# First GLU layer as 26 products of 4x4 by 4x2 blocks, with weight sums made during the first chunk and streamed from DRAM

## The chip, the core and the metric

The kernel runs on one core of a Trainium2 chip. The core has five engines that run side by side: TensorE (PE in the profile), VectorE (DVE), ScalarE (ACT), GpSimd (POOL) and SyncE (SP), which here only issues DMAs. Each engine works through its own queue strictly in order. The metric is the time of one execution on the device in microseconds, the median of several runs.

## The reference, cut to what matters

A linear attention block feeds a gated feed-forward layer, all in fp32 (the weights arrive as float64 and are converted on the chip).

```python
kv = np.einsum('bhsd,bhse->bhde', k, v)          # batch 8, heads 8, seq 576, head_dim 64
out = np.einsum('bhsd,bhde->bhse', q, kv)
out = out / sqrt(mean(out * out, -1) + 1e-6) * g_norm
x = out.transpose(0, 2, 1, 3).reshape(4608, 512)
gate = 1.0 / (1.0 + np.exp(-(x @ w_gate)))       # w_gate, w_val: 512 x 1536
val = x @ w_val
result = gate * val @ w_out                      # w_out: 1536 x 512
```

## The kernel before, in words

The 4608 tokens go through in nine chunks of 512 (G, NG). For each chunk c a first layer makes `h = sigmoid(gate) * val` and a second layer multiplies h with w_out. Everything lies in the transposed form that TensorE wants: xT holds 512 model dimensions as four tiles of 128 partitions, h holds 1536 hidden dimensions as twelve tiles.

**Chunk 0** (from the string `order` at L602 to L1096) starts the pipeline: eight pairs of heads of attention, the conversion of the weights (18 units, L156 to L211, five VectorE and two ACT instructions each: twelve "gv" units with a gate and a value tile, six "wo" units), and plain matmuls (`plain`, L583, and `second`, L669). In `plain` the conversion steps of the next unit are recorded between the matmuls of this one, so that TensorE waits for a unit only if VectorE is late.

**First layer of chunks 1 to 8** (`first_layer_fast`, L761). For each f of six, a gate and a value column tile and their partners f + 6 are treated as a 2x2 block product in Strassen-Winograd form: six products of two tiles and 256 tokens each on both partners, and the seventh again as a smaller such scheme of seven matmuls of 128x128. The sums of weights (tws, txs) are made on GpSimd in chunks 0 and 1 (`w_sum` L751, `w_sums2` L742), kept in DRAM and loaded again for each later chunk (`load_sums` L737). The sums of x (`x_sums` L702, `x_sums2` L712) are eight VectorE instructions a chunk.

**Second layer.** In chunk 1 it is plain (`second_layer_plain` L993), while VectorE makes 18 sums of w_out (`w_forms` L968). From chunk 2 on (`second_layer_fast` L1009) it is a scheme of 26 products (`PRODUCTS` L908), each a sum over three blocks j. Its left factors are 28 sums of h tiles per block (`H_SUMS` L899, `h_sums` L943, all on GpSimd), its right factors sums of w_out, streamed through a ring (`load_w` L964). The results are combined on VectorE and ACT as each product is done: `finish` (L1037) reads a small text such as `o5=o5-C`, in which capital letters are PSUM regions.

**PSUM banks.** Five banks circulate in a queue `free` (L540, `take` and `give`): a product that opens a region takes the oldest free bank, a region's last reader gives it back.

**The order around the change.** `fill` is a queue of single steps; `slot()` (L339) runs the next one. It is called at fixed places between products, seven times per f in the first layer and once per product in the second. In it lies the feed of attention for a later batch (`feed(b)`, L345, run during chunk b - 1): `kv_mm` (k and v products on TensorE, 40 of them), `kv_copies` on ACT, `turn` (VectorE transposes of q), and twice `two_pairs`: `u_mm` (TensorE), `u_square` (ACT), two `u_sum` (VectorE), `u_root` (ACT), two `u_norm` (VectorE, the first with a reciprocal that reads the root), two `x_turn` (VectorE transposes, each followed by DMAs on SP that place x in xT). `idle` steps and `spread` (L464) set the distances. After the feed come the x sums of the next chunk (`sums_of`, L1075). `load_late(b)` (L108) loads k and v of a batch into h_more, on SP, at the end of a second layer; in the kernel before, that of batch 2 is in the middle of chunk 0.

GpSimd's own queue holds the h sums, one addition per f, and the DMA issues of the weight sums and of the ring.

Of the kernel before, what the change touches and what calls it, by code (L numbers as in the profile page):

```python
# [10 lines left out]
FP32 = mybir.dt.float32  # L11
# [9 lines left out]
def kernel(  # L21
# [46 lines left out]
    NT = G // P  # L68

# [58 lines left out]
    units = [("gv", f) for f in range(NFT)] + [("wo", f) for f in range(0, NFT, 2)]  # L128
# [15 lines left out]

    def words(u):
        t = staged[u].rearrange("p i f -> p (i f)").bitcast(U32).rearrange("p (n two) -> p n two", two=2)
        return t[:, :, 0], t[:, :, 1]
# [8 lines left out]
    def convert(u):  # L156
# [4 lines left out]
        def s0():  # L161

            t = w1[:, f] if kind == "gv" else w2[:, f:f + 2, :]
            if kind == "gv":
                for i, name in enumerate(("wg", "wv")):
                    w[name, f] = t[:, i].rearrange("p (m f) -> p m f", m=NMT)
            else:
                for i in range(2):
                    w["wo", f + i] = t[:, i]
            d["m"] = m = t.rearrange("p i f -> p (i f)")  # L170
            vec.tensor_scalar(out=m.bitcast(U32), in0=words(u)[1], scalar1=0x000FFFFF, scalar2=None,
                              op0=ALU.bitwise_and)
# [5 lines left out]
        def s1():  # L178


            d["p"] = p = raw.tile([P, UW], U32, tag="cz", name="cz", bufs=2)
# [45 lines left out]
    w1 = const.tile([P, NFT, 2, DM], FP32, name="w1")  # L227
# [117 lines left out]
    def feed(b):  # L345

        early = b == 2
# [100 lines left out]
        if b > 2:  # L448
            steps += [(PE, idle)] * 6
        steps.append((PE, kv_mm))  # L450
        for i in range(2 * NC):
            for rs in ((0, 1), (2,)):
                steps.append((ACT, lambda i=i, rs=rs: kv_copies(i, rs)))

        u, *rest = two_pairs(n0)
        steps += turns_of(n0 + 1) + [u] + rest[:1] + [(PE, idle)] * (3 if b > 2 else 0) + turns_of(n0 + 2) + rest[1:]

        steps += [(PE, idle)] + turns_of(n0 + 3) + [(PE, idle)] * (2 if b > 2 else 0)
        return steps + two_pairs(n0 + 2) + [(PE, idle)] * 4
# [3 lines left out]

    def spread(steps, at):  # L464

        n = 0
        for engine, step in steps:
            while engine == DVE and n < 7 * NF2 and n % 7 not in at:
                fill.append(idle)
                n += 1  # L470
            fill.append(step)
            n += 1
# [6 lines left out]
    N3 = NF2 // 2  # L479
# [13 lines left out]

    def sg_tile():
        return sb.tile([P, G], FP32, tag="sg", name="sg", bufs=6)
# [87 lines left out]
    def plain(c, f, ps):  # L583

        blk = Plain(c, f, ps)
        for at in range(2 * NMT):
# [3 lines left out]
            convert_step(f + 1, at)  # L590
# [24 lines left out]
    for token in order.split():  # L615
# [3 lines left out]
        if name == "b":  # L619
            if f not in blks:  # L620
# [6 lines left out]
                blks[f] = Plain(0, f, ps)  # L627
# [9 lines left out]
        elif name == "M":  # L637
            nc.vector.tensor_tensor(out=gv_tile(0, f), in0=copies[f, 1], in1=copies[f, 0], op=ALU.mult)
# [11 lines left out]
        else:  # L650
            a[f][steps[name]]()
            if token == f"Q{NE - 1}":
# [3 lines left out]
                h_more = hp.tile([P, N3, 3 * NT, P], FP32, name="h_more")  # L656
    late.extend([blks[3].gate, blks[3].end])
    for f in range(4, NFT):
# [5 lines left out]
        if f == NFT - 2:  # L664
            load_late(2)
# [13 lines left out]
    raw_ctx.__exit__(None, None, None)  # L679

# [8 lines left out]
    NK = NMT // 2  # L689
    h1, h2 = slice(0, GH), slice(GH, G)  # L690
    tt = nc.vector.tensor_tensor
    sx, tw = {}, {}


    sx2, tw2 = {}, {}

    q1, q2 = slice(0, P), slice(P, GH)

    def quarters(c):
        return {(i, j): xT[c][:, NK * (j - 1):NK * j, GH * (i - 1):GH * i] for i in (1, 2) for j in (1, 2)}  # L700

    def x_sums(c):  # L702
        a = quarters(c)
        sx[c] = s = sums.tile([P, 3, NK, GH], FP32, tag="sx", name="sx", bufs=1)
        return [
            lambda: tt(out=s[:, 0], in0=a[2, 1], in1=a[2, 2], op=ALU.add),
            lambda: tt(out=s[:, 1], in0=s[:, 0], in1=a[1, 1], op=ALU.subtract),
            lambda: tt(out=a[2, 1], in0=a[1, 1], in1=a[2, 1], op=ALU.subtract),
            lambda: tt(out=s[:, 2], in0=a[1, 2], in1=s[:, 1], op=ALU.subtract),
        ] + x_sums2(c, a[1, 2])  # L710

    def x_sums2(c, a):  # L712
        sx2[c] = s = sums.tile([P, 3, P], FP32, tag="sx2", name="sx2", bufs=1)
        a11, a12, a21, a22 = a[:, 0, q1], a[:, 1, q1], a[:, 0, q2], a[:, 1, q2]
        return [
            lambda: tt(out=s[:, 0], in0=a21, in1=a22, op=ALU.add),
            lambda: tt(out=s[:, 1], in0=s[:, 0], in1=a11, op=ALU.subtract),
            lambda: tt(out=a21, in0=a11, in1=a21, op=ALU.subtract),
            lambda: tt(out=s[:, 2], in0=a12, in1=s[:, 1], op=ALU.subtract),
        ]  # L720

    def places(c, f):

        if c > 1 and f % 2 == 0:
            free_ = w1[:, :, 1, 0:NK * P]
            return free_[:, 0:8].rearrange("p (i e) n -> p i e n", e=2), free_[:, 8:10]
        return tws, txs

    def name_sums(c, f):
        t, x = places(c, f)  # L730
        for i in (1, 2, 3, 4):
            for e in range(2):
                tw[f + NF2 * e, i] = t[:, i - 1, e].rearrange("p (m c) -> p m c", m=NK)
            j, r = divmod(i - 1, 2)
# [403 lines left out]
```

## Time and profile before

| what | value |
|---|---|
| median of 3 runs | 1068.87 us (1067.32 to 1069.75) |
| the profiled execution | 1070.65 us, span 1068.8 us, granted TensorE clock 0.998 |
| VectorE, ACT, GpSimd busy | 600.7, 322.2, 504.3 us |
| chunk 0 | 0 to 160.2 us |
| chunk 1: first layer, plain second layer | 160.2 to 242.8, 242.8 to 284.0 us |
| chunks 2 to 6 | 284.0 to 851.0 us |
| chunks 7 and 8 (no feed in them) | 851.0 to 958.4, 958.4 to 1063.8 us |
| DMA | 184.5 MB, of it 119.6 MB on GpSimd's queue |

The page of the profile has one line of busy time per engine, then groups of instructions by source line, and the chain of work that ended last. The timeline lists start, duration, engine, source line, operation, tiles and count; a bracket at the end tells how long the engine stood idle before and what released it. Windows give busy time per engine in a stretch, in the order PE, PEld, DVE, ACT, POOL, then the granted clock and the DMA share. A matmul in fp32 appears as two records. Starts of TensorE records that follow each other without a gap show the rate; the duration of one record is longer, because they overlap.

### The profile page before, as it was taken

What the parts mean: (1) busy time and instruction counts of PE and PEld (TensorE: products, weight loads), DVE (VectorE), ACT (ScalarE), POOL (GpSimd) and SP (SyncE); (2) the same over time, 40 slices, a digit from 0 to 9 for tenths busy, and PEclk for the clock granted to TensorE, in tenths of its full rate; (3) what the DMA queues carried; (4) which work ended last, traced back from release to release, by engine and by line L of the source; (5) the groups of instructions that cost most, each with busy time, mean ns of one, the idle gap of its engine ahead of it and who ended that gap; (6) DMA issues with size and microseconds to landing.
All of it is one profiled execution on the core that took longest, in us unless ns stands there. A gap on an engine that the chain in (4) does not pass through costs nothing.

```text
span 1068.8 us, 19454 instructions
## 1 busy us (share of the span) xinstructions
PE 1052.3 (98%) x7334; PEld 858.2 (80%) x7334; DVE 600.7 (56%) x1340; ACT 322.2 (30%) x772; POOL 504.3 (47%) x972
## 2 busy tenths in 40 slices
PE   8999999999999999999999999999999999999998
PEld 7544448884688888888888788888888888888886
DVE  4887765566445555564557355555465555535542
ACT  4654324330142403331243224331334032202220
POOL 0000045782246842675166724682368427852762
PEclk9999999999999999999999999999999999999999
DMA  9944712346754686348733793358535833473214
GB/s 258 257 158 158 245 61 98 112 150 209 275 183 151 196 268 210 110 139 266 216 110 125 227 283 123 132 171 272 167 122 174 257 117 99 132 257 115 99 47 156
DMA packets 97533, 184.52 MB, mean 173 GB/s; under 512 B 29216, under 2 KB 68384, under 8 KB 94752
## 3 DMA queue, kind: packets, MB, share of 16 engines
q0 software_dynamic: 27168, 119.55, 33.6%
q1 hardware_dynamic: 70016, 63.66, 20.6%
q8 instruction: 58, 0.95, 0.4%
q14 instruction: 35, 0.29, 0.1%
q10 hardware_dynamic: 256, 0.07, 0.0%
HBM read 151.78 MB, written 24.38 MB: 165 GB/s over the span
## 4 chain that ended last, share of the span: by engine, by line
PE 87%; DMA 5%; POOL 4%; DVE 2%; issue 1%; ACT 0%; SPq 0%; POOLq 0%; DVEq 0%
PE mm L766 44%; PE mm L1034 15%; PE mm L571 7%; PE mm L770 7%; PE mm L999 4%; PE mm L670 4%; DMA xT<-xTs 3%; PE at L399 2%; PE at L358 1%; POOL tws L757 1%; POOL h_more L944 1%; DVE sg L1047 1%; PE at L571 1%; DMA w_ring<-kept 1%; PE two L295 1%
## 5 line engine op out<-in xcount | busy, mean ns | idle before, releaser
L766 PE MATMUL mm<-xT,w 128*128 128x256 f32 x720 | 177.5, 380 | 0.0
L766 PE MATMUL mm<-sx,w 128*128 128x256 f32 x720 | 177.1, 379 | 0.0
L766 PEld LDWEIGHTS mm<-xT,w 128*128 128x128 f32 x720 | 133.4, 190 | 17.7 <-issue 1.0
L766 PEld LDWEIGHTS mm<-sx,w 128*128 128x128 f32 x720 | 132.1, 190 | 15.2
L785 DVE TENSOR_TENSOR h<-mm,sg 128x256 f32<-128x256 f32 x96 | 40.8, 425 | 147.6 <-PE mm L766 147.6
L766 PE MATMUL mm<-sx,tws 128*128 128x256 f32 x432 | 111.1, 380 | 1.6 <-issue 1.6
L766 PE MATMUL mm<-xT,tws 128*128 128x256 f32 x432 | 112.5, 383 | 0.0
L858 POOL TENSOR_TENSOR sg<-sg 128x256 f32<-128x256 f32 x48 | 34.8, 726 | 149.6 <-ACT sg L857 141.8
L1034 PE MATMUL mm<-w,h 128*128 128x256 f32 x390 | 91.0, 379 | 0.0
L757 POOL TENSOR_TENSOR tws<-w 128x256 f32<-128x256 f32 x24 | 17.9, 768 | 152.0 <-DVE w L205 145.4
L944 POOL TENSOR_TENSOR h<-h 128x128 f32<-128x128 f32 x189 | 88.2, 479 | 2.8
L804 ACT ACTIVATE sg<-sg 128x256 f32<-128x256 f32 x96 | 40.0, 416 | 163.7 <-DVE sg L803 163.4
L813 DVE TENSOR_TENSOR h<-h,sg 128x256 f32<-128x256 f32 x192 | 86.1, 469 | 0.0
L766 PEld LDWEIGHTS mm<-xT,tws 128*128 128x128 f32 x432 | 77.8, 190 | 9.4
L766 PEld LDWEIGHTS mm<-sx,tws 128*128 128x128 f32 x432 | 75.9, 191 | 8.7 <-issue 1.8
L1034 PEld LDWEIGHTS mm<-w,h 128*128 128x128 f32 x390 | 74.1, 190 | 10.0
L779 ACT COPY sg<-mm 128x256 f32<-128x256 f32 x96 | 36.0, 375 | 138.2 <-PE mm L766 124.3
L1047 DVE TENSOR_TENSOR sg<-sg,mm 128x256 f32<-128x256 f32 x77 | 31.1, 418 | 82.7 <-PE mm L1034 82.4
L571 PE MATMUL mm<-xT,w 128*128 128x512 f32 x176 | 77.4, 594 | 0.0
L966 POOL DMA_DIRECT2D w_ring<-kept x90 | 49.6, 552 | 51.5 <-PE mm L1034 51.2
L944 POOL TENSOR_TENSOR h_more<-h 128x128 f32<-128x128 f32 x126 | 59.8, 480 | 29.0 <-DVE h L813 25.7
L1034 PE MATMUL mm<-w_ring,h_more 128*128 128x256 f32 x300 | 71.3, 382 | 2.1 <-issue 2.1
(132 smaller groups left out, 1796.3 us busy)
## 6 DMA issues: line engine op xcount, KB each, us to landing
w_ring<-kept POOLq DMA_DIRECT2D x90, 384.0 KB, 5.1
w<-kept POOLq DMA_DIRECT2D x21, 1024.0 KB, 6.1
tws<-kept POOLq DMA_DIRECT2D x21, 1024.0 KB, 5.2
w<-kept POOLq DMA_DIRECT2D x36, 384.0 KB, 5.1
out_dram<-sg SPq DMA_DIRECT2D x110, 64.0 KB, 3.3
q<-in_q_dram SPq DMA_DIRECT2D x24, 288.0 KB, 3.8
st<-in_moe_w_gate_dram SPq DMA_DIRECT2D x12, 512.0 KB, 5.5
st<-in_moe_w_val_dram SPq DMA_DIRECT2D x12, 512.0 KB, 6.1
```

The source lines that it names most:

```text
L571: nc.tensor.matmul(self.ps[i], w[("wg", "wv")[i], self.f][:, m, :], xT[self.c][:, m, :], start=(m == 0), stop=(m == NMT - 1), skip_group_c ...
L670: nc.tensor.matmul(ps[t], gv[0, f][:, P * t:P * t + P], w["wo", f], start=(f == 0), stop=(f == NFT - 1), skip_group_check=True)
L766: nc.tensor.matmul(ps, wt[:, m, :], xs[:, m, :], start=(new and m == 0), stop=(m == NK - 1), skip_group_check=True)
L770: nc.tensor.matmul(ps, wt, xs, start=new, stop=True, skip_group_check=True)
L785: tt(out=d["h"][:, h1], in0=d["pb"], in1=d["sg"][:, h2], op=ALU.add)
L804: nc.scalar.activation(out=d["sg"][:, h2], in_=d["sg"][:, h2], func=AF.Sigmoid)
L813: tt(out=d["h"][:, h], in0=d["h"][:, h], in1=d["sg"][:, h], op=ALU.mult)
L944: return [lambda v=v, x=x, sign=sign, y=y: nc.gpsimd.tensor_tensor(out=h_form(v, j), in0=h_form(x, j), in1=h_form(y, j), op=ALU.add if sig ...
L966: nc.gpsimd.dma_start(out=ring(i), in_=kept3[i % NS].rearrange("p (j n) -> p j n", j=N3))
L999: nc.tensor.matmul(ps, gv[c, f][:, tok[t]], w2[:, f, :], start=(f == order_[0]), stop=(f == order_[-1]), skip_group_check=True)
L1034: nc.tensor.matmul(regions[name][1], h_form(hv, j), ws[:, j], start=(new and j == 0), stop=(j == N3 - 1), skip_group_check=True)
L1047: tt(out=o[out_], in0=o[x], in1=o[y], op=ALU.add if sign == "+" else ALU.subtract)
```

## The change

The first layer takes the same scheme of 26 products that the second layer has. A block j (three of them) joins the tiles f = 2j, 2j + 1, 2j + 6, 2j + 7: four column tiles of the gate and four of the value weights. The four tiles of the model dimension and the four hidden tiles are the 4x4 left factor, for gate and value side by side (`g`), and x, as four dimension tiles by two halves of the tokens, is the 4x2 right factor. Each product is two matmuls of 128x128 weights with 256 tokens, for gate and value, which fill one PSUM bank side by side. The combinations thus work on 128x512 instead of 128x256, with the texts of `PRODUCTS1`, which also hold the sigmoids (`s0` to `s3`) and the multiplies of gate and value (`o4*o0` and so on), on GpSimd for blocks 0 and 1 and on VectorE for block 2.

The weights are converted in the order of the blocks (`F_ORDER`). In chunk 0, as soon as the four units of a block are converted and used, GpSimd makes 28 sums of 128x256 (`w1_sums`), partly in the place of the raw weights, partly in h_more, and writes the 26 factors to DRAM in two halves of 13 (`kept1`). From chunk 1 on they are streamed back as "granules" of half a block, 128 x 3328 values (1.7 MB), through three places in the old w1.

```diff
+    F_ORDER = [2 * j + NF2 * g + e for j in range(NF2 // 2) for g in range(2) for e in range(2)]
...
-        if b > 2:
-            steps += [(PE, idle)] * 6
+        steps += [(PE, idle)] * (5 if b > 2 else 10)
         steps.append((PE, kv_mm))
...
-            for rs in ((0, 1), (2,)):
-                steps.append((ACT, lambda i=i, rs=rs: kv_copies(i, rs)))
+            steps.append((ACT, lambda i=i: kv_copies(i, range(3))))
...
-        return steps + two_pairs(n0 + 2) + [(PE, idle)] * 4
+        return steps + two_pairs(n0 + 2) + [(PE, idle)] * 3
...
+    X_SUMS = ((10, 1, 5, -1, 7), (9, 1, 0, 1, 4), (12, 1, 3, -1, 9), (14, -1, 2, -1, 9), (8, 1, 5, -1, 6),
...
+    PRODUCTS1 = (("A", 8, 4, ""), ("B", 18, 10, ""), ("C", 9, 1, ""), ("E", 23, 12, "o5=A"), ("A", 24, 14, "o4=C"),
+                 ("C", 26, 16, "o3=B o1=A"), ("B", 25, 19, "o1=o1+B"), ("A", 33, 9, "t9=E t9=t9+A t8=C"),
+                 ("C", 30, 6, "o5=o5-C"), ("F", 27, 13, "t0=F"), ("B", 19, 25, "t0=B-t0"),
+                 ("H", 42, 3, "t9=t9-H o4=o4-t9"), ("G", 36, 7, "t1=G"), ("F", 35, 24, "t1=F-t1"),
+                 ("D", 20, 15, "o2=D o2=o2+t0"), ("E", 16, 22, "o7=t1-E"), ("G", 2, 23, "o1=G-o1"),
+                 ("I", 41, 11, "o5=o5+t1 o0=t9+t0"), ("D", 22, 20, "o0=o0+I s0 o1=o1-I"), ("E", 37, 21, ""),
+                 ("E", 40, 7, "s1 o5*o1"), ("H", 14, 18, "o3=o3+D o3=o3+E s3"), ("J", 39, 3, ""),
+                 ("J", 32, 17, "o2=J-o2 s2"), ("D", 31, 8, "t8=t8+D"),
+                 ("K", 43, 2, "o4=o4+K o7=o7-t8 o4*o0 o6=H+t8 o6*o2 o7*o3"))
...
+            eng = nc.vector if j == N3 - 1 and n < 10 else nc.gpsimd
...
+        for v in W_ORDER:
+            x, sign, y = SUMS[v]
+            nc.gpsimd.tensor_tensor(out=form(w_at[v]), in0=form(w_at[x]), in1=form(w_at[y]), op=op_of(sign))
...
+    def load_granule(g):
+        if g < N_GRAN:
+            nc.gpsimd.dma_start(out=granule(g), in_=kept1[g // 2 % N3, g % 2])
...
+    def w1_step(j):
+        steps = w1_sums(j)
+        next(steps)
+        if j:
+            load_granule(j - 1)
+        for _ in steps:
+            pass
...
-        if f == NFT - 2:
-            load_late(2)
+        if f % 4 == 3:
+            w1_step(f // 4)
...
+            for i, (name, hv, wv, steps) in enumerate(PRODUCTS1):
+                new = name not in regions
+                if new:
+                    i_ = free.popleft()
+                    regions[name] = i_, pair(bank(i_))
+                for g in range(2):
+                    nc.tensor.matmul(regions[name][1][:, g], w1_form(g0 + i // HALF, hv)[:, g], xf[c][wv],
+                                     start=(new and g == 0), stop=True, skip_group_check=True)
+                combine(o, regions, steps, nc.vector if j == N3 - 1 else nc.gpsimd)
+                give_all(regions, LAST1, i)
+                if i % 2:
+                    slot()
+                for _ in range(2 if i % HALF == HALF - 1 else 1):
+                    if h_fill:
+                        h_fill.popleft()[1]()
+                if i % HALF == HALF - 1 and (i < HALF or j < N3 - 1):
+                    load_granule(g0 + i // HALF + 3)
...
+        for eng, step in list(h_fill):
+            if eng is nc.vector:
+                step()
+        on_pool = deque(step for eng, step in h_fill if eng is nc.gpsimd)
...
+    flush()
+    load_late(2)
...
-            spread(feed(c + 1), (1, 2, 3, 4, 5) if c == 1 else (2, 3, 4, 5))
+            fill.extend(step for _, step in feed(c + 1))
```

`combine` is the old `finish` as a function of its own, with sigmoids and multiplies added; `give_all` gives back the regions whose last reader was this product. The x sums of a chunk are now 18 instructions of 128x256 on VectorE (`X_SUMS`), in the order in which the products need them; with 39 slots in a first layer the feed's last six steps fall into the second layer, and the x sums behind them. In the second layer the ten first h sums of block 2 move from GpSimd to VectorE, GpSimd's are taken two per product instead of three, and the ring of w_out sums keeps its seven places (two of them raw weights). The tile ring `sg` has five tiles in chunk 0 and eight later, before six.

## The prediction

> **What bounds the kernel now.** I read the page's engine and chain parts first, then the windows of one regular chunk, the chain in order of time, and last the timeline around a chunk's end.
>
> ```profile
> PE 1052.3 (98%) x7334; PEld 858.2 (80%) x7334; DVE 600.7 (56%) x1340; ACT 322.2 (30%) x772; POOL 504.3 (47%) x972
> ...
> PE 87%; DMA 5%; POOL 4%; DVE 2%; issue 1%; ACT 0%; SPq 0%; POOLq 0%; DVEq 0%
> ```
> ```profile
> 626.00:738.00 112.00, 111.73 (x897) 99.42 (x896) 60.45 (x151) 34.70 (x89) 60.54 (x120) 1.00 0.58 185
> ```
> In this chunk TensorE (first pair) is busy 111.73 of 112 us at clock 1.00; VectorE 60.5, GpSimd 60.5. So only fewer matmul columns shorten a chunk, and any new TensorE wait lengthens it in full. The chain gives the price of columns:
> ```profile
> 630.63 1.73 PE mm L766 x8
> 632.58 2.59 PE mm L766 x12
> 635.39 4.32 PE mm L766 x20
> 642.55 1.73 PE mm L766 x8
> ```
> 20 records in 4.32 us: 0.216 us each. Each fp32 matmul is two records, so 256 columns cost 0.432. One f takes 642.55 - 630.63 = 11.92 us, for 24 matmuls of 256 columns (10.37) and 7 of 128; those cost 1.55 / 7 = 0.22, so the small ones waste nothing.
>
> **TensorE work.** Before, the first layer costs 6 x 11.92 = 71.5 us a chunk. After: 3 blocks x 26 products x 2 matmuls x 0.432 = 67.4. The gain is 4.1 a chunk, 33 over eight. The second layer stays at 26 x 3 x 0.432 = 33.7, a feed at 2.2 + 2 x 1.73 = 5.7. With a feed a chunk is 106.8, without one 101.1. Before, chunks 2 to 6 run from 283.96 to 851.02, 113.4 each; 7 and 8 take 107.4 and 105.4. If nothing waited, those seven chunks would win 40 us. What remains is waits.
>
> **VectorE prices.** A product's 0.86 us of TensorE is followed 0.28 later by its reader (matmuls from 692.21, VectorE at 693.35). New is the 128x512 combination, 21 a block. Bounds: 0.69 busy (L579), or less with overlap:
> ```profile
> 717.03 1.42 DVE L417 TENSOR_TENSOR sqs<-at,ms 128x576 f32<-128x576 f32 x2
> ```
> Two 576-column ops in 1.42: the first holds 0.67, so 512 columns about 0.60. I take 0.60, and 0.73 when it reads the op just before (L706 to L707). A block is 13 us in 22.5 of TensorE, so the average fits. But 15 of the 21 come after product 12, with the feed's ops among them and five PSUM banks handed out in the order of their release: the next block's first four products A, B, C, E take the banks of E, J, D and H, which VectorE gives back with `o3+E`, `J-o2`, `t8+D` and `H+t8`. ACT has 9 copies of 0.585 and 4 sigmoids of 0.62 a block, 7.8 of 22.5 us, and hides beside TensorE; if it fell behind by the two products between a copy and the next use of its bank (1.7 us), that cover would be gone, and only the table load in the next paragraph comes near. Block 0's end has no feed op between its combinations and costs nothing: H's bank is back at 15.8 where E wants it at 16.1.
>
> **The waits, by walking the queues of a chunk with feed.** t = 0 is product 13's start.
> - *Block 1 to block 2.* VectorE reaches `o3=o3+E` at 10.1. Then comes the feed's reciprocal, which waits for ACT's root, itself behind s3 and a table load:
> ```profile
> 714.12 1.28 ACT L411 ACT_TABLE_LOAD   x1
> ```
> s3 10.8, load 12.0, root 12.4; norm ends 13.4. Queued behind it: `t8+D` (14.0), `o4+K`, `o7-t8`, `H+t8` (15.8). TensorE starts block 2 at 11.2; its third product needs D's bank (wait 1.1), its fourth H's (0.9). Wait 2.0; with contention (below) 2.5.
> - *Block 2 to the second layer.* The multiplies are on VectorE here (0.60 each). u_mm, behind product 15, shifts the end to 12.96. Six dependent ops follow K (13.25 to 16.9), a norm (17.9), then sum 18. Three first products over two blocks plus one cover 3.0. The next needs `o7*o3`, the one after sum 18 at 18.1: wait 1.7, with contention 2. Without feed the end is 11.2, `o7*o3` 15.2: wait 1.0.
> - *x sums.* Now 18 a chunk, from the eighth product of the second layer on. Behind the norm and ten h sums, moved from GpSimd to VectorE (0.2 to 0.28 each by L866, up to 0.65 where GpSimd's own sums alternate with them, so 4.6 in all), and the second norm, x_turn starts at about 23. Before:
> ```profile
> 721.48 8.78 SPq L434 DMA_DIRECT2D xT<-xTs  x11
> ...
> 734.98 0.69 DVE L706 TENSOR_TENSOR sx<-xT 128x512 f32<-128x512 f32 x1 [4.95 <-DMA xT<-xTs]
> ```
> Twelve issues on SP (11 here, one at 729.66) take 9.4 us, and the first sum starts 4.1 after the last. So the first x sum starts near 37, while TensorE would reach product 14 near 33.5. That product needs A's bank, freed by `t9+A` queued just behind the waiting x sum: wait 2.6 to 4.8, I take 3.7. Before, the combinations were already past.
> - *kv.* load_late goes on SP behind the stores, and kv_mm was 19.1 us into the chunk:
> ```profile
> 743.86 0.40 SPq L117 DMA_DIRECT2D h_more<-in_k_dram  x1
> ...
> 757.29 2.09 PE L358 MATMUL at<-h_more 128*64 128x64 f32 x64
> ```
> The chunk starts at 738.14, the loads at +5.7, the last issue ends +12.7, landing 5 more: +17.7. After, kv_mm comes behind 16 products, +13.8, its last part at +15.5: wait 2.
>
> Queued behind the waiting reciprocal and x sum are the combinations that free banks, and behind kv_mm all of TensorE; that is why each wait is charged in full. Sum 2.5 + 2 + 3.7 + 2 = 10.2: 117.0 a chunk, **+3.6, five times = +18**. Bounds of the sum: 4 (x and kv in time) to 14. Chunks 7 and 8 have no feed: 102.5 each, **-7.7**.
>
> **Chunk 0 and chunk 1.** GpSimd now makes 84 sums of 128x256 while VectorE converts weights. Alone one holds 0.70 (x2 in 1.41). The trace has one stretch of both:
> ```profile
> 146.68 2.31 POOL L757 TENSOR_TENSOR tws<-w 128x256 f32<-128x256 f32 x2 [145.37 <-DVE w L205]
> 147.30 1.10 DVE L707 TENSOR_TENSOR sx<-sx,xT 128x512 f32<-128x512 f32 x1
> 148.33 1.21 DVE L708 TENSOR_TENSOR xT<-xT 128x512 f32<-128x512 f32 x1
> ```
> VectorE's 0.69 became 1.1 to 1.2, GpSimd's 0.70 became 1.15: some 0.5 per VectorE op. A converted unit has three ops with two SBUF inputs (L192, L196, L203) and two plain ones: +1.5 to +2.5, on 0.28 + 0.65 + 5.1 = 6.0 against TensorE's 6.87 a unit. So 0.7 to 1.7 of TensorE wait in about 7 of 8 units: 8, plus 1 in the second layer: **+9**; lower bound 0 (GpSimd yields), upper 16. It hides nowhere, since TensorE waits for each unit. The Trainium skill, page "SBUF — State Buffer", section "Who interferes with whom", says why: a VectorE op with two SBUF inputs and a GpSimd op that reads SBUF exclude each other for a whole instruction. By it each of five ops would lose up to a whole 0.70, or 3.5 a unit, and chunk 0 up to 18; the rows say 0.5, and the sum goes by the rows.
>
> GpSimd does one sum between two conversions, so block 2's sums, which need unit 11, end near 168 and the kept1 writes near 180; granules 1 and 2 (1.7 MB; unseen, between 6.1 for 1 MB and 10 by its size) land about when chunk 1 asks, at +11 and +22. load_late(2) waits for the same h_more; kv_mm there is at +22. I put 3 on these waits together (0 to 8). Chunk 1 loses its 5.4 of waits for tws (82.6 against 71.5 + 5.7) and 4.1 of columns, gains 1.5 at block ends: -8 + 3 = **-5**. w_forms lie beside the plain second layer's 41.2 us as before.
>
> Later granules have 22.5 us from release to use, twice their load; GpSimd's h sums (28 x 0.45 a block) and multiplies (between 0.73 and 1.46) fit in 22.5. Both cost nothing, unless that queue falls 10 us behind. Block order and the sg ring of five add no instruction.
>
> **Sum:** 9 - 5 + 18 - 7.7 = +14. The profiled execution took 1070.65 (span 1068.8), the median 1068.87; on the median: **1083**.
>
> **Rivals.**
> - *The columns win.* For: 33 us of columns are certain, VectorE averages well under TensorE, and the block-end waits rest on ops I have only by interpolation. Against: the order of the queues. With 4 us of waits a chunk (110.8): 5 x -2.6 - 8 - 3 = -24, **1045**. It decides at 6.6 us of waits a chunk.
> - *Contention everywhere.* GpSimd's sums hold the conversions fully (+16), granules come late (+5 more), and SBUF-only combinations lose 0.5 each, waits 14: 5 x 7.4 = +37, net +50: **1119**. Against: GpSimd is idle half the time in first-layer blocks.
> - *No change:* waits eat exactly the columns, or the sums' cost does: **1069**.
>
> **Chances.** Forecast (slower, 1072 to 1100) 0.43, columns win 0.35, contention 0.16, none 0.06. 0.2% is about what a measurement here can tell: faster 0.35, same 0.06, slower 0.59. The range reaches into both sides: 1043 to 1109; the forecast's own is 1072 to 1100.
>
> **What would show it.** Right: TensorE idle before product 14 of the second layer, ended by VectorE behind an x sum that waited for xT; an idle at block 1's end with a reciprocal waiting for ACT; kv_mm waiting for h_more's DMA; conversions L200/L204/L211 over 1.5 us while GpSimd sums. Wrong: chunks 2 to 6 under 111 us with TensorE over 97% busy, or chunk 0 ending before 163.

## The result and the profile after

The changed kernel takes 1139.97 us (median of 4 runs, 1131.28 to 1145.44), the kernel before 1068.28 beside it: ratio 1.066, 95% interval 1.059 to 1.074. It is slower, and by far more than forecast (1083, range up to 1109). The profiled execution took 1142.67 us, span 1140.9.

The page of the changed kernel: busy time, granted clock in 40 slices, and the chain.

```profile
PE 1050.9 (92%) x6854; PEld 831.2 (73%) x6854; DVE 708.8 (62%) x1210; ACT 349.7 (31%) x604; POOL 557.8 (49%) x897
...
PEclk9999997799989999899989998999989999999999
...
PE 59%; DMA 14%; DVE 10%; POOL 8%; ACT 3%; issue 3%; SPq 2%; DVEq 0%; POOLq 0%; ACTq 0%
```

TensorE has 480 records fewer, as planned, yet it is no longer the bound: 92% of the span in place of 98%, and DMA holds 14% of the chain in place of 5%. The clock row is new: it has dips, where before it was 9 throughout. What TensorE waited for in the changed kernel (total us, times, longest):

```profile
PE at L371 <- DMA h_more<-in_v_dram: 26.4, 6, 6.3
PE mm L898 <- DMA w<-kept: 14.8, 1, 14.8
PE at L365 <- DMA h_more<-in_v_dram: 9.4, 6, 4.8
PE mm L999 <- DVE h L862: 8.4, 7, 1.4
PE mm L898 <- DVE temps L870: 5.2, 5, 1.0
PE at L365 <- POOL h L862: 5.1, 1, 5.1
...
PE mm L999 <- DVE h_more L725: 2.3, 5, 0.5
```

Lines L365 and L371 are kv_mm: 40.9 us of waits with the one that the profile puts down to GpSimd. One is a granule of weight sums (L898, w from kept). The block-end waits that VectorE causes (L862, L870, L725) are at most 1.4 each. By stages, against the forecast on this execution's own time (1070.65 + 14):

| part | forecast | measured | difference |
|---|---|---|---|
| chunk 0 | 169.2 | 163.4 | -5.8 |
| chunk 1 | 118.8 | 149.1 | +30.3 |
| chunks 2 to 6, each | 117.0 | 123.6 | 5 x 6.6 = +33 |
| chunks 7 and 8, each | 102.5 | 102.4, 102.5 | 0 |

The differences add up to 57.5 of the 58 us by which the forecast was short. One regular chunk (the columns as in the window of the kernel before):

```profile
559.00:682.00 123.00, 113.75 (x839) 96.95 (x838) 74.12 (x144) 37.92 (x68) 59.36 (x107) 0.96 0.57 192
```

TensorE is idle for 9 of 123 us, at a mean clock of 0.96. VectorE has 74 us of work in it, GpSimd 59: neither is near full. Where chunk 4 (562.46 to 685.22) stops, in the timeline of TensorE:

```profile
576.36 2.08 PE L365 MATMUL at<-h_more 128*64 128x64 f32 x64
578.38 0.33 PE L371 MATMUL at<-h_more 64*64 64x64 f32 x4
583.89 0.69 PE L371 MATMUL at<-h_more 64*64 64x64 f32 x12 [5.18 <-DMA h_more<-in_v_dram]
584.51 5.63 PE L898 MATMUL mm<-xs,w 128*128 128x256 f32 x16
589.99 1.03 PE L898 MATMUL mm<-xT,w 128*128 128x256 f32 x4
```

From the start of kv_mm to the next product pass 8.15 us, where kv_mm needs 2.4: 5.7 of wait, not 2. And behind it stands a cost that the forecast didn't have: 16 records from 584.51 to 589.99, 5.48 us, which at 0.216 each take 3.46. Two windows that begin at 576 and 586 show clocks of 0.78 and 0.88. The wait thus costs about 8 us. Its cause is on SP, where load_late's issues come behind the stores:

```profile
559.58 7.25 SPq L510 DMA_DIRECT2D out_dram<-sg  x11
567.20 0.40 SPq L118 DMA_DIRECT2D h_more<-in_k_dram  x1
...
573.23 1.44 SPq L123 DMA_DIRECT2D h_more<-in_v_dram  x2
```

Issue begins 4.7 us into the chunk and ends 12.2 in, as forecast; but the last 64 KB pieces of v take 9.4 us to land (median), not 5. The very last one, issued at 574.07, shares its time with a 1.7 MB granule that GpSimd asks for at 574.14; the first row is the kernel before in the chunk that the forecast walked (issued at 750.16, beside a load of 1 MB):

```profile
h_more<-in_v_dram SPq DMA_DIRECT2D x1, 64.0 KB, 8.9
...
w<-kept POOLq DMA_DIRECT2D x1, 1664.0 KB, 9.5
h_more<-in_v_dram SPq DMA_DIRECT2D x1, 64.0 KB, 9.8
```

In each of chunks 3 to 6 this piece is issued between 0.1 us ahead of the granule and 0.6 behind it, takes 9.1 to 10.4 us, and lands 0.2 to 0.4 after the granule does. The piece before it in chunk 4, issued 0.9 us ahead of the granule, landed in 4.7.

The block ends are as forecast. Block 1 to block 2, VectorE and TensorE:

```profile
621.70 0.27 DVE L422 RECIPROCAL ms<-ms 128x18 f32<-128x18 f32 x1 [1.72 <-ACT ms L418]
...
623.41 1.13 PE L898 MATMUL mm<-xT,w 128*128 128x256 f32 x4 [1.04 <-DVE temps L870]
...
625.21 3.07 PE L898 MATMUL mm<-xs,w 128*128 128x256 f32 x13 [0.67 <-DVE h L870]
```

The reciprocal waits for ACT, and two products wait 1.04 and 0.67 (forecast: 1.1 and 0.9). Before the second layer the two waits are 1.43 and 0.47. The x sums do wait for xT, as foreseen, but nobody waits for them:

```profile
667.23 0.42 DVE L838 TENSOR_TENSOR xs<-xT 128x256 f32<-128x256 f32 x1 [4.70 <-DMA xT<-xTs]
667.57 0.41 DVE L870 TENSOR_TENSOR temps<-temps,mm 128x256 f32<-128x256 f32 x1
```

Product 14 (the first is 0) starts at 669.7, and its bank is back at 668.0, when the second row ends: in time.

In chunk 0 a conversion on VectorE, alone in the kernel before and beside a sum in the changed one:

```profile
79.63 1.22 DVE L196 SCALAR_TENSOR_TENSOR cz<-st,cz 128x1024 uint32<-128x1024 uint32 x1
...
89.64 1.75 DVE L204 SCALAR_TENSOR_TENSOR cz<-st,cz 128x1024 uint32<-128x1024 uint32 x1
```

GpSimd's sums in chunks 0 and 1, and the granule they hold up:

```profile
141.50 2.85 POOL L744 TENSOR_TENSOR w<-w 128x256 f32<-128x256 f32 x2
...
164.70 1.40 POOL L744 TENSOR_TENSOR w<-w 128x256 f32<-128x256 f32 x2
...
180.32 0.72 POOL L744 TENSOR_TENSOR h_more<-h_more,w 128x256 f32<-128x256 f32 x1
180.99 0.56 POOL L763 DMA_DIRECT2D w<-kept  x1
```
```profile
189.55 3.41 PE L898 MATMUL mm<-xT,w 128*128 128x256 f32 x8 [14.78 <-DMA w<-kept]
```

A sum takes 1.4 us beside conversions (first row) and 0.70 when they are over (second row). The last one ends at 181, where I had sized 168, and only then is granule 1 asked for. The eight records behind that wait take 3.2 us instead of 1.7: half rate.

**Theory** after this: no engine is the bound; the loss is waits for DMAs that are issued too late (k and v in every feed chunk; granules, k and v in chunk 1, behind the sums), and each long wait costs some 2 us more because the clock falls. **Rivals:** contention of VectorE and GpSimd throughout; waits that only move when one is taken away; transfers that are slow in themselves, wherever they are queued.

### The profile page after: what moved, and what is told of

It reads as the page before. It is cut to its first block, busy times and chain, and to the rows that moved or that the text cites. A ratio compares the mean times of both kernels' runs of the same rounds, so it can differ in the third digit from the quotient of the medians.

```text
span 1140.9 us, 18090 instructions
## 1 busy us (share of the span) xinstructions
PE 1050.9 (92%) x6854; PEld 831.2 (73%) x6854; DVE 708.8 (62%) x1210; ACT 349.7 (31%) x604; POOL 557.8 (49%) x897
## 4 chain that ended last, share of the span: by engine, by line
PE 59%; DMA 14%; DVE 10%; POOL 8%; ACT 3%; issue 3%; SPq 2%; DVEq 0%; POOLq 0%; ACTq 0%
PE mm L898 32%; PE mm L999 16%; DMA h_more<-in_v_dram 7%; POOL w L744 4%; PE mm L968 4%; DMA out_dram<-sg 4%; DVE sg L870 3%; POOL h_more L744 3%; DVE h L870 3%; PE mm L568 2%; DMA kept<-h_more 2%; PE at L406 2%; DMA kept<-w 2%; DVE h L862 1%; SPq L118 1%
## 5 line engine op out<-in xcount | busy, mean ns | idle before, releaser
L898 PE MATMUL mm<-xs,w 128*128 128x256 f32 x1536 | 372.4, 390 | 3.6 <-DVE h L870 3.3
L898 PEld LDWEIGHTS mm<-xs,w 128*128 128x128 f32 x1536 | 297.5, 195 | 51.0 <-DVE h L870 5.4
L898 PE MATMUL mm<-xT,w 128*128 128x256 f32 x960 | 237.1, 384 | 21.5 <-DMA w<-kept 14.8
L898 PEld LDWEIGHTS mm<-xT,w 128*128 128x128 f32 x960 | 183.3, 192 | 52.4 <-issue 15.9
L870 DVE TENSOR_TENSOR sg<-sg,mm 128x512 f32<-128x512 f32 (+1 forms) x169 | 99.0, 606 | 161.6 <-PE mm L898 88.4
L862 POOL TENSOR_TENSOR h<-h,sg 128x512 f32<-128x512 f32 x64 | 86.1, 1364 | 179.1 <-ACT sg L859 140.1
L725 POOL TENSOR_TENSOR h<-h 128x128 f32<-128x128 f32 x189 | 94.6, 513 | 71.1 <-DVE h_more L725 68.6
L866 ACT COPY temps<-mm 128x512 f32<-128x512 f32 (+1 forms) x124 | 64.4, 542 | 199.4 <-PE mm L898 108.4
L870 DVE TENSOR_TENSOR sg<-mm,sg 128x512 f32<-128x512 f32 (+1 forms) x62 | 38.7, 624 | 95.0 <-PE mm L898 77.7
L763 POOL DMA_DIRECT2D w<-kept x48 | 27.1, 564 | 118.6 <-PE mm L898 116.7
L999 PE MATMUL mm<-w,h_more 128*128 128x256 f32 x342 | 82.6, 393 | 1.9 <-DVE h_more L725 1.9
L935 POOL DMA_DIRECT2D w<-kept x90 | 57.5, 640 | 49.5 <-PE mm L999 48.1
L568 PE MATMUL mm<-xT,w 128*128 128x512 f32 x176 | 78.4, 595 | 1.9 <-DVE w L211 1.9
L999 PEld LDWEIGHTS mm<-w,h_more 128*128 128x128 f32 x342 | 67.1, 197 | 13.1 <-DVE h_more L725 3.5
L870 DVE TENSOR_TENSOR temps<-mm,temps 128x512 f32<-128x512 f32 (+1 forms) x62 | 39.0, 629 | 51.3 <-PE mm L898 42.9
L870 DVE TENSOR_TENSOR temps<-temps,mm 128x512 f32<-128x512 f32 (+1 forms) x93 | 58.1, 624 | 15.7 <-PE mm L999 7.0
L568 PEld LDWEIGHTS mm<-xT,w 128*128 128x128 f32 x176 | 32.3, 190 | 40.7 <-issue 40.3
```

The costliest lines, as they stand in the source:

```text
L568: nc.tensor.matmul(self.ps[i], w[("wg", "wv")[i], self.f][:, m, :], xT[self.c][:, m, :], start=(m == 0), stop=(m == NMT - 1), skip_group_c ...
L725: ops.append((eng, lambda v=v, x=x, sign=sign, y=y, eng=eng: eng.tensor_tensor(out=h_form(v, j), in0=h_form(x, j), in1=h_form(y, j), op=op ...
L763: nc.gpsimd.dma_start(out=granule(g), in_=kept1[g // 2 % N3, g % 2])
L862: mult.tensor_tensor(out=o[x], in0=o[x], in1=o[y], op=ALU.mult)
L866: nc.scalar.copy(out=o[out_], in_=o[expr])
L870: tt(out=o[out_], in0=o[x], in1=o[y], op=ALU.add if sign == "+" else ALU.subtract)
```

## The experiments

Times are medians; ratios are to the kernel before, measured beside them. A chunk's time is from its first matmul to that of the next.

**1. Stores behind load_late** (chunks 2 to 5).

```diff
+                elif i > 22 and c + 2 < B:
+                    held.append(t)
...
         load_late(c + 2)
+        for t in held:
+            store(c, t, rows[t])
```

> In chunks 2 to 5 the last eight stores of the second layer (products 24 and 25) are issued on SP behind load_late instead of ahead of it; nothing is left out. Theory: kv_mm's wait (5.95 us in chunk 4) is mis-sized SP order: 16 stores hold the queue 13 us, so k and v land at +21.7 us of the chunk. With 8 stores fewer ahead they land some 6.5 us earlier, kv_mm waits under 1 us in chunks 3 to 6, and the low clock behind the wait (0.66, worth 2.0 us) goes with it: -8 us a chunk, four chunks, -32 (between -24 and -36). Rival 1, a wait only moves to the next place where VectorE is late: -10 or less, with block 1 to block 2 growing from 2.1 to over 5. Rival 2, it is the transfer (a granule of 1.7 MB at the same time) and not the queue: the issue is earlier but the landing is not, kv wait still over 4, -8 or less.

1111.51 us, ratio 1.040 (1.036 to 1.044): -28. Chunks 3 to 6 take 114.5 on average (122.8 before the edit): -8.3 each. TensorE in its chunk 4:

```profile
567.20 2.08 PE L365 MATMUL at<-h_more 128*64 128x64 f32 x64
569.22 0.46 PE L371 MATMUL at<-h_more 64*64 64x64 f32 x16
569.61 3.72 PE L898 MATMUL mm<-xs,w 128*128 128x256 f32 x16
```

No wait, and the 16 records take 3.55 us. The theory's size holds, and rival 1 falls: block 1 to block 2 still waits 1.04 and 0.67, so nothing moved there. The theory's reason is half of it. In chunk 4 the last piece of v lands 13.0 us into the chunk, not 21.4; only 2.4 of these 8.4 us are an earlier issue (the theory had 6.5), the other 5.9 are the landing itself:

```profile
h_more<-in_v_dram SPq DMA_DIRECT2D x1, 64.0 KB, 3.8
```

In chunks 3 to 6 of this run the piece is issued 2.5 to 4.0 us ahead of the granule and lands in 3.7 to 4.2. So rival 2 named a real part of the cause: the place in SP's queue decides whether the last piece is issued clear of the granule. No run moved the granule alone.

**2. The feed later.**

```diff
-        steps += [(PE, idle)] * (5 if b > 2 else 10)
+        steps += [(PE, idle)] * 10
```

> Ten idle steps ahead of kv_mm in every feed, not five: kv_mm comes 10 products (8.6 us) later, and all of the feed behind it. Nothing is left out. Theory: kv wait gone in chunks 2 to 6 (-6 each), with it its clock loss (-2); the first norm falls past block 1's end, so that wait falls from 2.1 to under 0.5; the second pair of heads falls deeper into the second layer, and the x sums start 4 us later, so that a wait ahead of product 14 appears (0 to 4). Net -6 to -10 a chunk, -30 to -50. Rival, the wait moves: the feed's end is flushed at the end of the second layer and the x sums of the next chunk are late for its first product, +3 to +6 a chunk, net -10 to +5 in all.

1080.29 us, ratio 1.010 (1.008 to 1.013): -60, more than expected. Chunks 3 to 6 take 110.4, chunk 2 115.9: below the 113.4 of the kernel before on average (111.5). The waits for k and v are gone in chunks 3 to 6 (0.39 left in chunk 2), and so are both block-end waits; 0.3 and 0.67 for ACT within blocks 1 and 2, and 0.3 to 0.7 for VectorE near block 2's end, are new. The edit also shows the forecast's x wait, in chunk 2 alone and four products later (the bank is freed behind another x sum). VectorE, then TensorE:

```profile
413.80 0.76 DVE L838 TENSOR_TENSOR xs<-xT 128x256 f32<-128x256 f32 x2 [7.91 <-DMA xT<-xTs]
414.47 0.42 DVE L870 TENSOR_TENSOR temps<-mm,temps 128x256 f32<-128x256 f32 x1
...
414.95 2.93 PE L999 MATMUL mm<-w_ring,h 128*128 128x256 f32 x6 [3.84 <-DVE temps L870]
```

The mechanism is real; in the changed kernel it costs 0.7, in chunk 2.

**3. TensorE kept busy in the wait.**

```diff
+            for _ in range(24 if b > 2 else 0):
+                nc.tensor.matmul(full[:, 2, 0:P], ident, ident, start=True, stop=True)
```

> 24 matmuls of the identity (128 columns, into a bank that nobody reads) stand between kv_mm's main products and its last part, in chunks 2 to 6; nothing is left out. They cost some 5 us of TensorE and fill the 6 us wait. Theory of the clock: the granted clock falls after an idle, and 16 records then cost 5.48 us for 3.46. With TensorE busy in the wait the clock stays near 1.0 and the chunk is 1 to 2 us shorter: -5 to -10 in all. Rival, the fall of the clock is not caused by the idle (or costs nothing): 0, or +5 where the fillers outlast the wait.

1135.27 us, ratio 1.061 (1.057 to 1.065). The interval overlaps that of the changed kernel, so the total proves nothing; the chunks do. TensorE in its chunk 4:

```profile
580.30 5.62 PE L369 MATMUL at<-ident 128*128 128x128 f32 x48
585.86 0.46 PE L374 MATMUL at<-h_more 64*64 64x64 f32 x16
586.25 3.72 PE L901 MATMUL mm<-xs,w 128*128 128x256 f32 x16
```

The stop is as long, but filled with work that nobody needs, and the 16 records behind it take 3.55 us, not 5.48. Chunks 3 to 6 average 120.0 (122.8): -2.8 with more work done. In chunk 2, where kv_mm's main part waits as well, the fillers only add (131.9 for 126.9). So the fall of the clock is caused by the idle, and costs about 2 us behind a wait like this one. The Trainium skill, page "TensorE: Matmul & The Clock Gate", section "HAM oscillation — how this bites in real kernels", warns of idle gaps over some 3.4 us that leave the next matmuls at half rate. The 5.18 and 14.78 us gaps agree. But in chunk 4, waits of 1.43 and 0.47 before the second layer were also followed by 20 records in 6.1 us instead of 4.3 (clock 0.83 from 650 to 660), so shorter gaps can be enough; no run here settles which.

**4. No sums of weights.** It leaves out the 84 sums; zeros are written in their place.

```diff
-            nc.gpsimd.tensor_tensor(out=form(w_at[v]), in0=form(w_at[x]), in1=form(w_at[y]), op=op_of(sign))
+            nc.gpsimd.memset(form(w_at[v]), 0.0)
```

> Leaves out part of the computation: GpSimd writes zeros with 84 memsets in place of the 84 sums of weights of the first layer; the DMA writes to DRAM and all reads stay. Theory: the sums run 1.7 us beside conversions, not 1.15, and end 13 us later than sized, which is why granule 1 (14.8 us) and load_late(2) (14 us) are late in chunk 1. Without them chunk 0 ends near 160 (163.4 now), the first layer of chunk 1 takes 75 to 80 us (107.8 now): -28 to -35 in all. Rival 1, the waits of chunk 1 come from the DMAs (writes of 6 MB and granules on one queue): chunk 0 -3, chunk 1 -10 or less. Rival 2, contention on VectorE is the larger part: chunk 0 itself -8 or more.

1101.27 us, ratio 1.028 (1.024 to 1.033): -39. Chunk 0 ends at 159.7 (163.4), and the window of chunk 1's first layer is clean:

```profile
159.69:235.00 75.31, 74.33 (x681) 64.32 (x679) 48.22 (x79) 31.35 (x56) 13.43 (x13) 1.00 0.52 172
```

75.3 us for 107.8, TensorE 99% busy at clock 1.00, with every DMA still there. So the waits of chunk 1 come from the sums, which start the transfers late; started earlier, the same transfers hold nothing up. The sums cost chunk 0 only 3.7 us. Both rivals fall. The run takes away the sums' own time and their contention with the conversions together; it doesn't tell them apart.

**5 to 7. What holds the sums up.** Run 5 gives block 1's sums their own places, run 6 asks for granule 1 earlier, run 7 does both.

```diff
-            return more[:, s_ - 4 * NMT:s_ - 4 * NMT + n].rearrange("p s n -> p (s n)")
+            p0 = s_ - 4 * NMT
+            p0 += 10 if j == 1 and p0 < 8 else 0
+            return more[:, p0:p0 + n].rearrange("p s n -> p (s n)")
```
```diff
+            if j == 2 and n == 10:
+                load_granule(1)
...
-        if j:
-            load_granule(j - 1)
         for _ in steps:
             pass
+        if j == 1:
+            load_granule(0)
```

> Block 1's weight sums of chunk 0 get places of their own in h_more (10 to 17, then 8 and 9) instead of those that block 0's factors are still being written out from; nothing is left out. Theory: GpSimd's end of the sums (181 us, sized at 168) is made of slow sums beside conversions and of waits for the factors' own DMAs (6.48 at 102 us, 2.15 at 159). These two waits go, the sums end near 173, granule 1 and load_late(2) move up with them: first layer of chunk 1 some 8 us shorter (107.8 to about 100), the rest as it was: -8 in all. Rival, contention alone sets the pace (the sums catch up only when VectorE stops converting): -3 or less.

> Granule 1 of chunk 1 is loaded after ten of block 2's 28 sums instead of behind all of them, and granule 0 behind block 1's writes instead of ahead of them; nothing is left out. Theory: chunk 1's wait is for the end of the sums and writes, not for one load: granule 1's wait (14.8) goes, but granule 2 lies where block 2's factors are, and k and v of batch 2 too, so that TensorE stops there instead, 11 or so later: net -3 to -6 (the writes no longer wait 4.4 + 1.3 behind a load). Rival, the wait is that load's place in GpSimd's queue only: -13 to -15.

> Both edits of chunk 0 and 1 together (own places for block 1's sums, granule 1 early), the feed as in the changed kernel; nothing is left out. Theory: the sums end near 168, granule 1 lands in time, granule 2 lands near 187, as it is wanted; k and v of batch 2 land near 197, kv_mm still waits some 9 us in chunk 1. First layer of chunk 1 85 to 92 us (107.8 now), in all -16 to -22. Rival, each wait of chunk 1 is replaced by the next one: first layer of chunk 1 still over 98, -10 or less.

Run 5: 1138.77, ratio 1.066 (1.063 to 1.069): no difference, the rival's side. Its GpSimd doesn't wait at 104 any more, and gains almost nothing by it. The first two rows are the changed kernel, the others run 5:

```profile
100.89 1.07 POOL L744 TENSOR_TENSOR h_more<-w 128x256 f32<-128x256 f32 x1
...
110.17 3.53 POOL L744 TENSOR_TENSOR h_more<-w 128x256 f32<-128x256 f32 x3 [6.48 <-DMA kept<-h_more]
...
101.86 1.08 POOL L746 TENSOR_TENSOR h_more<-w 128x256 f32<-128x256 f32 x1
...
142.56 1.60 POOL L746 TENSOR_TENSOR h_more<-h_more,w 128x256 f32<-128x256 f32 x1
144.10 0.73 POOL L766 DMA_DIRECT2D w<-kept  x1
```

Block 1's 28 sums run from 101.86 to 144.1, 1.51 us each; in the changed kernel they ran from 100.9 to 145.4 with the wait of 6.48 in between, 1.36 each without it. So 4.2 of the 6.5 us came back as slower sums while VectorE was still converting, and the last sum of all ends at 179.5 for 181.0. That the conversions pace them is the likely reading; no run changed the conversions.

Run 6: 1132.28, ratio 1.060 (1.058 to 1.062): -8. Granule 1's wait is gone, but kv_mm in chunk 1 still stops (the profile names nothing for the first of these waits):

```profile
200.25 1.12 PE L365 MATMUL at<-h_more 128*64 128x64 f32 x16 [7.45 <-issue]
...
207.08 1.12 PE L365 MATMUL at<-h_more 128*64 128x64 f32 x16 [4.30 <-DMA h_more<-in_v_dram]
...
210.45 2.07 PE L900 MATMUL mm<-xT,w 128*128 128x256 f32 x4
```

Its k and v go to h_more, which the factors of block 2 are still being written out from. I had named granule 2 as the first to be late; it was k and v. The wait moves, as the theory said, but only in part: granule 1's 14.8 us go, kv_mm's waits in chunk 1 grow from 10.5 to 12.6, and one of 3.5 for ACT is new. The 8 us lie between theory and rival. Run 7: 1133.11, ratio 1.060 (1.058 to 1.063): -7 where -16 to -22 was expected. Its first layer of chunk 1 takes 92.1, the upper end of the theory (15.7 less), but in that profiled execution alone (1127.03); the median kept only 7. It is a miss in size, and it doesn't differ from run 6.

**8 to 10. The parts together.** Run 8 joins run 7 to a later feed (10 idle steps; 14 for batch 2, where the last three are dropped and the one ahead of the last transposes). Run 9 takes batch 2's changes back. Run 10 is run 9 with 8 steps for batches 3 to 7, and run 1's held stores.

```diff
-        steps += [(PE, idle)] * (5 if b > 2 else 10)
+        steps += [(PE, idle)] * (10 if b > 2 else 14)    # run 8; run 9: 10; run 10: (8 if b > 2 else 10)
...
-        steps += [(PE, idle)] + turns_of(n0 + 3) + [(PE, idle)] * 2
-        return steps + two_pairs(n0 + 2) + [(PE, idle)] * 3
+        steps += [(PE, idle)] * (b > 2) + turns_of(n0 + 3) + [(PE, idle)] * 2
+        return steps + two_pairs(n0 + 2) + [(PE, idle)] * (3 if b > 2 else 0)
```

The last two lines are run 8's alone.

> Both edits of chunk 0 and 1, and the feed later: ten idle steps ahead of kv_mm for batches 3 to 7, fourteen for batch 2 (and three of its later idle steps fewer). Nothing is left out. Theory: the waits add up and no engine is the bound: -60 from the feed, -18 and some -9 from chunk 1: 1045 to 1060 us, ratio to the kernel before 0.975 to 0.99, with chunks 2 to 6 near 110 us and chunk 1 near 122. That also is what the columns alone had promised. Rival, contention or clock holds the sum above the kernel before: 1068 to 1085.

> Ten idle steps ahead of kv_mm in every feed, own places for block 1's sums, granule 1 early; the fourteen steps of batch 2 are taken back. Nothing is left out. In the run with fourteen, chunk 1's plain second layer took 45.3 us (41.3 in all others) and chunk 2 121.3 (115.9 with the feed later alone). Theory: both come from the fourteen steps, whose feed, and all w_forms and x sums behind it, end too late: without them chunk 1 takes 92 + 41 and chunk 2 116: 1062 to 1066, ratio 0.993 to 0.998. Rival: they come from granules and sums of chunk 1 moved forward, and stay: 1067 to 1072.

> Eight idle steps ahead of kv_mm for batches 3 to 7 (ten for batch 2), the last eight stores of chunks 2 to 5 behind load_late, own places for block 1's sums, granule 1 early. Nothing is left out. Theory of waits: k and v land at +14, kv_mm asks at +19, no wait; the x sums of chunk 2 start 1.7 us earlier than with ten steps (wait 3.8 to 2); the norm falls 2.6 us earlier than with ten steps and 5 us later than block 1's end wants it with five, so the block-end wait stays under 1. 1058 to 1066, 0 to 5 below the run with ten steps. Rival: the block-end wait comes back (1.7 and 1.9 a chunk, five times): 1068 to 1080.

Run 8: 1069.63, ratio 1.002 (1.000 to 1.003), against 1045 to 1060 expected: a miss. Chunks 3 to 6 are at 110.1, but chunk 1 takes 133.3 (forecast 122) and chunk 2 121.3. Run 9: 1068.02, ratio 1.000 (0.999 to 1.002). Chunk 2 falls to 112.3 and chunk 1's plain layer to 41.3, as expected; but chunk 1's first layer is 96.5 (88.0). Windows of its chunk 1 show why:

```profile
186.00:197.00 11.00, 5.77 (x27) 4.75 (x25) 5.86 (x10) 2.49 (x4) 5.69 (x5) 0.93 1.01 384
197.00:207.00 10.00, 4.49 (x64) 3.86 (x64) 0.00 (x0) 0.00 (x0) 0.20 (x1) 0.50 1.02 356
207.00:217.00 10.00, 9.79 (x47) 8.28 (x48) 0.34 (x1) 5.90 (x14) 0.00 (x0) 0.73 0.00 1
```

TensorE waits 10.9 us in all at kv_mm, in the second window at clock 0.50, with the DMA engines full (share 1.0) until 207: block 2's factors out, granules in, k and v in, all at once.

Run 10: 1090.98, ratio 1.021 (1.019 to 1.023), worse than either theory said. Against run 9, chunks 4 to 6 lose 2.7 each (the second layer waits 0.96 and 0.42 again, the first 0.62 for ACT), chunk 2 loses 9.0 (kv_mm waits 3.4 for k and v of batch 3, which run 1's edit doesn't reach, and the clock drops to 0.76), chunk 3 6.4, of it 2.34 in a stop that the profile puts down to nothing. Together that is all of the 23.5 us between the two spans. Of chunk 3's stop the cause stays open.

**11. The later feed and no sums.** It leaves out the sums, as in run 4; the edits are those of runs 2 and 4.

> The feed later (ten idle steps) and no sums of weights together. Leaves out the sums of weights of the first layer (84 memsets of zero in their place), as the earlier run without sums; the DMAs stay. Theory: the two groups of waits are separate, so their gains add up: 1140 less 60 (feed) less 39 (sums) is 1041, and with chunk 0 at 160, chunk 1 at 116.6, chunks 2 to 6 near 111 the case in which the columns win is reached: 1038 to 1048. Rival, the two gains share a cause (the same waits, or the clock): 1055 or more.

1042.35 us, ratio 0.975 (0.973 to 0.977). The gains add up as expected (1041). Its page:

```profile
PE 1020.0 (98%) x6854; PEld 815.3 (78%) x6854; DVE 684.1 (66%) x1210; ACT 347.6 (33%) x604; POOL 484.8 (47%) x897
...
PEclk9999999999999999999999999999999999999999
```

TensorE is the bound again, at full clock, and the time is that of the forecast's rival "the columns win" (1045). This is no usable kernel, but it shows where the expected gain is: 26 us faster than the kernel before. Part of that is the sums' own cost (some 4 us of chunk 0, which ends at 159.5 here and at 164.0 in run 2); whether the rest can be had with the sums made in time, no run shows.

**12. Batch 2's k and v later, with the idle step kept.** As run 9, with this:

```diff
-        steps += [(PE, idle)] * (5 if b > 2 else 10)
+        steps += [(PE, idle)] * (10 if b > 2 else 14)
...
-        return steps + two_pairs(n0 + 2) + [(PE, idle)] * 3
+        return steps + two_pairs(n0 + 2) + [(PE, idle)] * (3 if b > 2 else 0)
```

> As the run with ten idle steps and both edits of chunk 0 and 1, but fourteen idle steps ahead of kv_mm of batch 2 and none behind its last transposes; the idle step ahead of the fourth pair's transposes stays, which was missing when chunk 1's plain layer took 45.3 us. Nothing is left out. Theory: kv_mm of chunk 1 waits 10.5 us there and the clock falls to 0.50; 3.4 us later it waits 6 to 7: chunk 1 some 4 to 7 us shorter (137.8 to about 132), chunk 2 as it was (112): 1060 to 1065, ratio 0.993 to 0.997. Rival: what chunk 1 wins, chunk 2 gives back, because batch 3's k and v and the x sums come as much later: 1067 to 1072.

1068.59, ratio 1.001 (1.000 to 1.003): the rival. Chunk 1 wins 5.2 (132.6 for 137.8), chunk 2 gives back 7.2 (119.5 for 112.3). Here a wait does move: the feed, the x sums and the sums of w_out stand in one queue of steps, chunk 1's plain layer gets 3.2 us longer (44.5 for 41.3), and in chunk 2 kv_mm waits 4.4 us for k and v of batch 3, which are loaded behind it (run 9: no wait there). No complete version tried beats the kernel before; runs 8, 9 and 12 equal it.

## Why the prediction failed

- **Columns, right.** Chunks 7 and 8, where nothing is fed, take 102.4 and 102.5 (forecast 102.5), a first layer 67.5 (67.4). (The forecast's "40 us" for seven chunks without waits is 44 by its own numbers; nothing rests on it.)
- **Block ends, right.** 2.1 and 2.3 us in chunk 4, for 2.5 and 2.0, with the reciprocal behind ACT as walked. The 0.60 for a 128x512 combination held: in a row of them that is the distance of their starts.
- **Signs.** Of those named in the forecast, the waiting reciprocal, the waiting kv_mm and the conversions over 1.5 us are there; the idle before product 14 is there in chunk 2 alone (0.7).
- **x sums, wrong by 3.7.** The walk had the first x sum 37 us after product 13's start and TensorE at product 14 after 33.5. In chunk 4 the first x sum came after 33.3, because the twelve issues on SP took 7.7 us for 9.4 and the data followed 2.5 after them for 4.1, and TensorE came after 35.7. In run 1, without the wait at kv_mm, it is 32.9 and 34.2, so TensorE's lateness is hardly needed for it to be in time.
- **kv, a failed step in chunks 2 to 6.** The sum had a wait of 2 us a chunk, from "landing 5 more". Five is the median of these pieces in the kernel before. The last piece, for which kv_mm waits, took 8.9 there in the very chunk of the walk, and its reader started 0.3 us after it landed. With 8.9 the walk gives 5.4. It took 9.8 in the changed kernel, and the wait cost 5.7; in chunk 2, behind the plain layer, 8.2.
- **A term that was missing, the failed step that decides chunks 2 to 6: the clock.** The forecast charged a wait with its own length. Those at kv_mm and ahead of the second layer cost about 2 us more each. Chunk 4 is 5.8 us over 117.0; 5.7 for 2 at kv_mm (+3.7), the clock behind it (+2.0) and behind the second layer's waits (+1.8), less the x wait (-3.7), name 3.8 of them. That the errors at kv_mm and at the x sums cancel is luck. The other 2 are small stops that I did not take apart.
- **"3 on these waits together (0 to 8)", the failed step in chunk 1.** Run 4 and the changed kernel put them at 107.8 - 75.3 = 32.5 us. The row of 1.15 us per sum was from a stretch in which VectorE's operations were half as wide (512 columns, for 1024 in a conversion); beside conversions a sum takes 1.05 to 1.7, 1.36 on average in block 1. I saw that granules and load_late(2) hang on the sums' end, but sized that end 13 us too early, and then added the waits of three loads as one.
- **Contention in chunk 0, too large.** +9 forecast, +3.2 measured; run 4 gives 3.7 for the sums. The price of the row held: an operation of 1.22 us takes up to 1.75 beside a sum, one of 0.69 takes 1.21, and VectorE is busy 141.5 us in chunk 0, for 120.8 without the sums. What was too large is what TensorE pays of these 21 us. The walk had 6.0 us of VectorE in a unit of 6.87; the kernel before shows 5.45. So a unit with sums beside it fills VectorE for 7.3, not quite 0.5 over TensorE's 6.87, and TensorE's waits for conversions (L568 behind L211) come to 1.9 us in all. The Trainium skill's rule on the shared port (page "SBUF — State Buffer", section "Who interferes with whom") says that one of the two operations is held for a whole instruction, whichever comes second; both sides are slower here, which agrees. The 18 took VectorE as the one held, in every operation, and with too little room.
- **The sign** was right for a reason that held: waits by queue order eat the columns (run 11, with hardly a wait and without the sums, is 26 us faster). The range failed because two waits were each sized from a row that was milder than the place it was used for, a median landing and a sum beside narrow operations.

The rival "contention everywhere" (1119; with chunk 1's -5 kept, its terms add up to 1114) came nearest to the time and had the wrong mechanism. In run 9, which makes all sums and every combination, chunks 3 to 6 take 110.1, where it had 120.8, and chunk 0 loses 3 to 4 us, where it had 16.

## What to carry to other kernels

When a change moves a consumer ahead on a tuned engine, list each DMA that it reads, with its place in its issuing queue, the large transfer that may meet it and its slowest landing (not the median), and treat the margin as the quantity to forecast; here 5 idle steps, or eight stores moved in a queue, were worth 60 and 28 of the 72 us lost. Price a TensorE wait of a few us at its length plus the slow matmuls behind it, and look for that in the granted clock. Work given to an idle engine in a busy stretch ends later than its price alone says, and everything that reads its results moves with it.

## What was not expected of the hardware

- After an idle of 5.18 us, 16 records took 5.48 us for 3.46; after 14.78 us, eight took 3.2 for 1.7; filling the idle with needless matmuls brought the 3.55 back. The windows around such waits show clocks of 0.50 to 0.88. Waits of 1.04 and 0.67 us at block 2's start left it at 1.00 (618 to 628), those of 1.43 and 0.47 ahead of the second layer didn't (0.83 from 650 to 660).
- A GpSimd sum of 128x256 takes 0.70 us alone and 1.05 to 1.7 beside conversions, which are slower too (1.22 to 1.75); when 6.5 us of waiting were removed, the sums gave 4.2 of them back (1.51 each for 1.36).
- A piece of 64 KB on SP's queue lands in 3.7 to 4.2 us when it is issued 2.5 us or more ahead of a 1.7 MB load on GpSimd's queue (run 1), and in 9.1 to 10.4, just after that load, when both are issued together (changed kernel, chunks 3 to 6).
